# Two raw input tiles transposed by a DMA from DRAM instead of on TensorE, in a gated mixer and MLP block

## The chip, the cores and the metric

The kernel runs on one core of one Trainium2 chip. A core has five engines with instruction queues of their own: TensorE (PE: matrix products and transposes, results in PSUM), VectorE (DVE), ScalarE (ACT), GpSimd (POOL) and SyncE (SP, which here only issues DMAs); sixteen DMA engines carry out what SP and ACT issue. The metric is the device time of one execution in microseconds (us), lower is better. PEld is TensorE's weight load, which overlaps its products.

## The reference

The input x is 2048 by 512, in bf16. With LN a layer norm without gain or bias over the last axis, and gelu in its tanh form:

```python
h  = gelu(LN(x) @ w1)              # 2048x512 @ 512x512
# channel quarters of h: shifted along the sequence by +1, -1, +2, -2 rows, zeros moved in
hs = concatenate([g0, g1, g2, g3], axis=-1) @ w2
x1 = x + hs
y  = x1 + gelu(LN(x1) @ w3) @ w4   # w3 512x1792, w4 1792x512
```

## The kernel before, in words

The 2048 rows are 16 tiles of 128 (row p*16+t is partition p of tile t), so a shift along the sequence is a step from one tile to another. Each product needs its input with channels on partitions, so every tile has to be transposed once for w1 and once more, after the second layer norm, for w3.

Two sorts of tiles are treated differently in the first layer. Tiles 0 to 5 are "raw" (R = 6): x itself is transposed and multiplied by w1 (m1r), and the layer norm is put on afterwards, on the product, from the column sums of w1 (cs) and the statistics of the tile (zr, g1r); the result hraw is then transposed by a DMA (th_t, two tiles at a time, into hT). Tiles 6 to 15 are normed first (st: statistics, ag: their aggregation, rs: the root on POOL, nm: the norm on DVE), transposed and multiplied in pairs (m1p, then gelu g1p or g1s on ACT, straight into hT).

There are two ways of transposing. On TensorE, `tp` does four 128x128 transposes a tile against an identity (line 357) into PSUM, and `ev` copies the bank to xnT (line 366). By DMA, `tdma` (line 377; td0_t in the first layer, td1_t in the second) takes a pair of tiles from SBUF to SBUF, issued on SP. Before the change, raw tiles 0 to 5 and the pairs 8 and 10 went through TensorE, and pairs 6, 12 and 14 through the DMA.

Then m2 (lines 463 and 478, in parts) multiplies the shifted windows of hT by w2, DVE adds x (x1, line 488), and the second layer goes over the tiles in the order 8 to 15, 0 to 7 (ORDER), four at a time: m3h (first four, in halves, line 520) and m3 (line 496) with w3, gelu, m4 with w4 (line 539) and the last addition (fin). Tile t of m2 reads its neighbours: m2_14 and m2_15 read tiles 0 and 1 of hT too, which come out of th_0.

The order on each engine is written out by hand in `firsts`, one list of names per engine; `arrange` keeps each list, and `emit` puts waits only where a tile is read or overwritten. Every DMA has a semaphore of its own. What stands in a list is done in that order, so an operation that waits holds everything behind it on its engine. The lists that matter here:

- PE: the raw transposes and their m1r run interleaved from 4 us on; after m1r5 come tp8 m1p6 tp10 m1p8 m1p10, then parts of m2 for tiles 8 to 11, then m1p12, m1p14 and the rest of m2, and the first m3h.
- DVE: st0_10 and st0_11 stand ahead of nm0_8 and nm0_9, and st0_12 and st0_13 ahead of nm0_10 and nm0_11.
- SP: x and w1, w2 in the order of first use; td0_6 waits for nm0_7, td0_12 for nm0_13, td0_14 for nm0_15, th_0 for g1r1, td1_8 for nm1_9. The first halves of w3 (ldw3a0 to 3, 256 KB each) are loaded in pairs between these, the second halves (ldw3b, 192 KB each) after td1_8.

The kernel is straight-line code: nothing of it loops on the chip.

Of the kernel before, what the change touches and what calls it, by code (L numbers as in the profile page):

```python
# [26 lines left out]
class Program:  # L27
# [7 lines left out]
    def add(self, eng, name, fn, reads=(), writes=(), dma=False):  # L35
        self.ops.append(Op(name, eng, fn, reads, writes, dma))
# [135 lines left out]
def bass_standalone__mixer_s_mlp__prompt_kernel(nc: bass.Bass, x, w1, w2, w3, w4, out):  # L172
# [10 lines left out]
    xd = x[0].rearrange("(p t) d -> p t d", t=NT)  # L183
# [4 lines left out]
    with ExitStack() as es:  # L188
# [5 lines left out]
        xnT = sb("xnT", [P, NT, DC, P], BF16)  # L194
# [52 lines left out]
        add = pr.add  # L247
# [4 lines left out]
        def bres(b, n, tag):  # L252
            return [(("ps", b + i), tag) for i in range(n)]
# [19 lines left out]
        def load_x(t, n, eng="sp"):  # L273
            add(eng, f"ldx{t}", lambda e: e.dma_start(x_sb[:, t : t + n, :], xd[:, t : t + n, :]),
                writes=[(("x", i), 0) for i in range(t, t + n)], dma=True)
# [72 lines left out]
        def tp(t, n, b, raw):  # L348
            src = x_sb if raw else xn
            rd = [(("x", i), 0) if raw else (("xn", i), 0) for i in range(t, t + n)]  # L350

            def f(e):
                ins = None
                for i in range(n):
                    for c in range(DC):
                        o = 1024 * b + (i * DC + c) * P
                        ins = e.transpose(psb[:, o : o + P], src[:, t + i, P * c : P * (c + 1)], ident[:])  # L357
                return ins

            add("pe", f"tp{t}", f, reads=rd + [("ident", 1)], writes=bres(b, 1, f"tp{t}"))  # L360

        def ev(t, n, b, eng="act"):
            src = psb[:, 1024 * b : 1024 * b + n * D]
            dst = xnT[:, t : t + n, :, :].rearrange("p t c s -> p (t c s)")
            if eng == "act":
                f = lambda e: e.activation(dst, src, ACT_F.Copy)  # L366
            else:
                f = lambda e: e.tensor_copy(dst, src)
            add(eng, f"ev{t}", f, reads=bres(b, 1, f"tp{t}"), writes=[(("xT", i), 0) for i in range(t, t + n)])


        def tdma(layer, t, n):
# [6 lines left out]
                reads=[dst_of(layer, i)[2:] for i in range(t, t + n)],  # L379
                writes=[(("xT", i) if layer == 0 else ("x1T", i), 0) for i in range(t, t + n)], dma=True)  # L380

        def tdma_h(t, n):
            add("sp", f"th_{t}",
                lambda e: e.dma_start(hT[:, t : t + n, :, 0:P].rearrange("p t j w -> p (t j) w"),
                                      hraw[:, t : t + n, :].rearrange("p t d -> p (t d)"), transpose=True),
                reads=[(("hraw", i), 0) for i in range(t, t + n)],
                writes=[(("hT", i), 0) for i in range(t, t + n)], dma=True)
# [13 lines left out]
        def m1r(t, b, c0=0, c1=DC):  # L401
            def f(e):
                ins = None
                for c in range(c0, c1):
                    ins = e.matmul(bank(b), xnT[:, t, c, :], w1_sb[:, c, :], start=(c == 0), stop=(c == DC - 1))  # L405
                return ins

            rd = [(("xT", t), 0)] + W1[c0:c1]
            if c0:
                rd += bres(b, 1, f"m1r{t}{c0}")  # L410
            end = f"{c1}" if c1 < DC else ""
            add("pe", f"m1r{t}{end}", f, reads=rd, writes=bres(b, 1, f"m1r{t}{end}"))

        def rc(t, b):
            add("act", f"rc{t}", lambda e: e.activation(yraw[:, t, :], bank(b), ACT_F.Copy),
                reads=bres(b, 1, f"m1r{t}"), writes=[(("yraw", t), 0)])
# [169 lines left out]
        load_w1(2, "act")  # L586
        load_w1(3, "sp")
        load_x(1, 1, "act")
        for t, n in ((6, 1), (7, 1), (2, 1), (8, 1), (3, 1), (9, 1), (10, 1), (4, 1), (11, 1), (5, 1), (12, 2), (14, 1), (15, 1)):
            load_x(t, n)  # L590
        for c in range(DC):
            load_w2(c)
# [7 lines left out]
            colsum(4, c)  # L600
        colsum_out(4)
        for t in range(R):
            tp(t, 1, 6 + t % 2, True)
            ev(t, 1, 6 + t % 2, "act")
            cuts = [0, 1, 2, 3, 4] if t == 0 else [0, 2, 4] if t == 1 else [0, 4]
            for c0, c1 in zip(cuts, cuts[1:]):
                m1r(t, YB[t], c0, c1)
            rc(t, YB[t])
# [37 lines left out]
        for t in range(0, R, 2):  # L646
            roots(0, t, 2)
            for i in (t, t + 1):
                zr(i)
                g1r(i)  # L650
            tdma_h(t, 2)
        for t in (8, 10):
# [7 lines left out]
            tdma(1, t, 2)  # L660

        firsts = {}
        firsts["pe"] = """wu tp0 cs0 cs1 m1r01 m1r02 tp1 m1r03 m1r0 cs2 tp2 m1r12 m1r1 cs tp3 m1r2 tp4 m1r3 tp5 m1r4 m1r5 tp8 m1p6
            tp10 m1p8 m1p10 m2_8a m2_9a m2_8 m2_9b m2_9 m2_10a m2_11a m1p12 m1p14 m2_10 m2_11 m2_12a m2_13a m2_12 m2_13 m2_14 m2_15""".split()
        firsts["act"] = """ldw10 ldw12 ldx1 table ev0 ev1 ev2 rc0 ev3 rc1 ev4 rc2 ev5 rc3 rc4 rc5 ev8 cse g1p6 ev10 g1p8 g1s10 g1s11
            g1r0 g1r1 g1p12 g1p14 g2h_0_0_0 g2h_0_0_4 g1r2 g1r3 g2h_0_0_8 g2h_0_0_12 g1r4 g1r5""".split()
        firsts["dve"] = """pada padb padc padd pade padf st0_0 st0_6 st0_7 ag0_6 ag0_7
            st0_8 nm0_6 nm0_7 st0_9 ag0_8 ag0_9 st0_10 st0_11 nm0_8 nm0_9 ag0_10 ag0_11
            st0_12 st0_13 nm0_10 nm0_11 ag0_12 ag0_13 st0_14 nm0_12 nm0_13 st0_15 ag0_14 ag0_15 st0_1 ag0_0 ag0_1
            nm0_14 nm0_15 zr0 zr1 x1_8 x1_9 st1_8 st1_9 ag1_8 ag1_9 st0_2 nm1_8 nm1_9 st0_3 ag0_2 ag0_3 x1_10 x1_11 st1_10  # L670
            st1_11 ag1_10 ag1_11 x1_12 nm1_10 nm1_11 x1_13 x1_14 x1_15 zr2 zr3 st0_4 st0_5 ag0_4 ag0_5 zr4 zr5
            st1_12 st1_13 ag1_12 ag1_13""".split()
        firsts["pool"] = """ident0 ident1 neghalf stz ste rs0_6 rs0_8 rs0_10
            rs0_12 rs0_14 rs0_0 rs1_8 rs0_2 rs1_10""".split()
        firsts["sp"] = """ldx0 ldw11 ldw13 ldx6 ldx7 ldx2 ldx8 ldx3 ldx9 ldx10 ldx4 ldx11 ldx5 ldx12 td0_6 ldx14 ldx15 ldw20 ldw21 ldw22 ldw23 td0_12 ldw3a0 ldw3a1 td0_14
            ldw3a2 ldw3a3 th_0 td1_8 ldw3b0 ldw3b1 ldw3b2 ldw3b3 td1_10 th_2 th_4 td1_12 td1_14 ldw4""".split()

        slots = [4, 0, 2]
        ns = [0]
# [110 lines left out]
```

## Time and profile before

| | |
|---|---|
| median of three runs | 137.16 us (136.78 to 137.19) |
| the profiled execution | 136.84 us, its span 134.9 us |
| TensorE busy | 131.8 us, 98% of the span, clock granted in full |
| DVE, ACT, POOL busy | 57.9, 47.6, 12.4 us |
| moved by DMA | 12.70 MB, of it 6.82 read from HBM and 2.10 written to it |
| 128x128 transposes on TensorE (L357) | 40: 24 of raw tiles, 16 of normed ones |

How to read it. The span goes from the first to the last instruction of the profiled execution. A group's line names the line of the kernel, engine, operation, what is written and read, and shapes. A matmul's busy time is longer than the distance to the next one, since they are pipelined: 128x512 products start 0.216 us apart and are shown as 0.379 long. The chain is followed back from the last instruction, from each to what released it. The DMA view gives for each issue the time from the issue to the landing, the moment at which the semaphore has its full count. A DMA share over 1 means more than one open packet per DMA engine.

### The profile page before, as it was taken

Reading aid. Unit: us, or ns where it says so; the run is one execution under the profiler, and the core shown is the slowest. Engines: PE = TensorE matmul, PEld = TensorE weight load, DVE = VectorE, ACT = ScalarE, POOL = GpSimd, SP = SyncE. Lnnn points to the kernel's source line nnn. Section 1 sums busy time; section 2 is a strip of 40 time slices with the busy share of each in tenths; the row PEclk is TensorE's granted clock in tenths of the full one; section 3 lists DMA queues with packets and bytes.
Section 4 is the critical chain, followed back from the end, with each engine's and each line's share of the span. In section 5 each row is a group of like instructions: output and inputs, shape, how many; then the busy total and the mean of one; then the engine's idle time right before and its main releaser. Section 6 shows DMA issues by size and latency. Waiting matters only on the chain.

```text
span 134.9 us, 1823 instructions
## 1 busy us (share of the span) xinstructions
PE 131.8 (98%) x737; PEld 69.8 (52%) x737; DVE 57.9 (43%) x135; ACT 47.6 (35%) x58; POOL 12.4 (9%) x25
## 2 busy tenths in 40 slices
PE   7999999999999999999999999999999999999993
PEld 2356867568885444444444444444444444444452
DVE  0499979999866786772222000122200002322222
ACT  3489873407963025551000555200066630000000
POOL 2023422220420012220000000000000000000000
PEclk9999999999999999999999999999999999999999
DMA  3988589774466973444112000011110001111121
GB/s 104 332 264 189 151 228 251 132 222 83 77 119 119 290 256 66 92 78 78 39 48 70 3 0 0 0 39 39 39 39 5 0 0 39 39 39 39 41 78 41
DMA packets 23512, 12.70 MB, mean 94 GB/s; under 512 B 15696, under 2 KB 22864, under 8 KB 23504
## 3 DMA queue, kind: packets, MB, share of 16 engines
q1 hardware_dynamic: 22928, 12.16, 35.8%
q10 hardware_dynamic: 576, 0.43, 1.1%
q8 instruction: 6, 0.10, 0.3%
q14 instruction: 2, 0.02, 0.0%
HBM read 6.82 MB, written 2.10 MB: 66 GB/s over the span
## 4 chain that ended last, share of the span: by engine, by line
PE 98%; DVE 0%; issue 0%
PE ps L539 36%; PE ps L496 27%; PE ps L520 9%; PE ps L437 6%; PE ps L463 6%; PE ps L405 4%; PE ps L478 4%; PE ps L562 2%; PE ps L357 2%; PE ps L393 1%; DVE o_sb L551 0%
## 5 line engine op out<-in xcount | busy, mean ns | idle before, releaser
L539 PE MATMUL ps<-w_sb,h2T 128*128 128x512 bf16 (+2 forms) x238 | 48.9, 367 | 0.0
L507 ACT ACTIVATE h2T<-ps 128x1024 bf16<-128x1024 f32 x21 | 21.5, 1023 | 46.2 <-PE ps L496 46.2
L551 DVE TENSOR_TENSOR o_sb<-ps,x_sb 128x512 bf16<-128x512 f32 (+2 forms) x17 | 11.2, 660 | 61.2 <-PE ps L539 61.2
L496 PE MATMUL ps<-x1nT,w_sb 128*128 128x512 bf16 x168 | 36.8, 379 | 0.0
L539 PEld LDWEIGHTS ps<-w_sb,h2T 128*128 128x128 bf16 x238 | 22.7, 98 | 26.0
L496 PEld LDWEIGHTS ps<-x1nT,w_sb 128*128 128x128 bf16 x168 | 16.5, 98 | 19.8
L291 DVE BATCH_NORM_STATS2 st<-x_sb 128x6 f32<-128x512 bf16 x32 | 20.6, 676 | 4.1 <-DMA x_sb<-in_x_dram 4.1
L302 POOL TENSOR_TENSOR rstd<-mv,neghalf 128x2 f32<-128x2 f32 x16 | 11.5, 718 | 46.6 <-DVE mv L296 46.5
L520 PE MATMUL ps<-x1nT,w_sb 128*128 128x256 bf16 x112 | 12.4, 273 | 0.0
L488 DVE TENSOR_TENSOR x_sb<-ps,x_sb 128x512 bf16<-128x512 f32 x16 | 10.6, 685 | 3.1 <-PE ps L463 2.1
L520 PEld LDWEIGHTS ps<-x1nT,w_sb 128*128 128x128 bf16 x112 | 11.0, 98 | 1.5
L531 ACT ACTIVATE h2T<-ps 128x1024 bf16<-128x1024 f32 (+1 forms) x8 | 7.1, 913 | 6.6 <-PE ps L520 6.6
L437 PE MATMUL ps<-xnT,w_sb 128*128 128x256 bf16 x80 | 9.2, 273 | 0.0
L463 PE MATMUL ps<-w_sb,hTf 128*128 128x512 bf16 x40 | 9.0, 379 | 0.0
L437 PEld LDWEIGHTS ps<-xnT,w_sb 128*128 128x128 bf16 x80 | 7.7, 98 | 1.2
L311 DVE TENSOR_SCALAR x1n<-x_sb,mv,rstd 128x512 bf16<-128x512 bf16 x16 | 5.9, 410 | 5.3 <-POOL rstd L302 5.3
L366 ACT ACTIVATE xnT<-ps 128x512 bf16<-128x512 bf16 (+1 forms) x8 | 5.6, 702 | 2.5 <-PE ps L357 2.4
L463 PEld LDWEIGHTS ps<-w_sb,hTf 128*128 128x128 bf16 x40 | 3.9, 98 | 4.5
L405 PE MATMUL ps<-w_sb,xnT 128*128 128x512 bf16 x24 | 6.2, 381 | 0.0
L478 PE MATMUL ps<-w_sb,hTf 128*128 128x512 bf16 x24 | 5.5, 379 | 0.0
L447 ACT ACTIVATE hTf<-ps 128x1024 bf16<-128x1024 f32 x4 | 4.1, 1023 | 3.4 <-PE ps L437 3.4
L296 DVE BATCH_NORM_AGGREGATE mv<-st 128x2 f32<-128x9 f32 x32 | 4.9, 184 | 0.0
(28 smaller groups left out, 37.2 us busy)
## 6 DMA issues: line engine op xcount, KB each, us to landing
out_dram<-o_sb SPq DMA_DIRECT2D x15, 128.0 KB, 1.8
w_sb<-in_w_dram SPq DMA_DIRECT2D x1, 1792.0 KB, 8.1
x_sb<-in_x_dram SPq DMA_DIRECT2D x13, 128.0 KB, 3.5
w_sb<-in_w_dram SPq DMA_DIRECT2D x4, 256.0 KB, 3.8
w_sb<-in_w_dram SPq DMA_DIRECT2D x6, 128.0 KB, 3.3
w_sb<-in_w_dram SPq DMA_DIRECT2D x4, 192.0 KB, 3.0
w_sb<-in_w_dram ACTq DMA_DIRECT2D x2, 128.0 KB, 3.5
x_sb<-in_x_dram SPq DMA_DIRECT2D x1, 256.0 KB, 3.5
```

Source lines behind the costliest of these rows:

```text
L291: add("dve", f"st{layer}_{t}", lambda e: e.bn_stats(st9[:, i, 0:6], src[:, t, :]), reads=[(r, 0)], writes=[(("st6", i), 0)])
L302: lambda e: e.tensor_tensor(rstd[:, i : i + n], mv[:, i : i + n, 1], neghalf[:, 0:n], ALU.pow),
L405: ins = e.matmul(bank(b), xnT[:, t, c, :], w1_sb[:, c, :], start=(c == 0), stop=(c == DC - 1))
L437: ins = e.matmul(dst, w1_sb[:, c, P * fc : P * (fc + 1)], xnT[:, t : t + 2, c, :], start=(c == 0), stop=(c == DC - 1))
L463: ins = e.matmul(bank(b), hTf[:, c0 : c0 + P], w2_sb[:, j, :], start=(j == 0), stop=(j == DC - 1))
L478: ins = e.matmul(bank(b), hTf[:, w[0] : w[0] + P], w2_sb[:, j, :], start=first and n == 0, stop=last and n == len(js) - 1)
L488: lambda e: e.tensor_tensor(x1_sb[:, t, :], bank(b), x_sb[:, t, :], ALU.add),
L496: ins = e.matmul(bank(b), w3_sb[:, c, P * fc : P * (fc + 1)], x1nT[:, 4 * q : 4 * q + 4, c, :], start=(c == 0), stop=(c == DC - 1))
L507: lambda e: e.activation(h2T[:, fc : fc + 2, q % 2, :], src, ACT_F.Gelu_apprx_tanh),
L520: ins = e.matmul(dst, w3_sb[:, c, P * (fc + i) : P * (fc + i + 1)], x1nT[:, t : t + 2, c, :], start=(c == 0), stop=(c == DC - 1))
L539: ins = e.matmul(ps[:, 512 * b : 512 * b + c1 - c0], h2T[:, fc, q % 2, P * i : P * (i + 1)], w4_sb[:, fc, c0:c1], start=(fc == 0), stop=(f ...
L551: lambda e: e.tensor_tensor(o_sb[:, k % 4, c0:c1], ps[:, 512 * b : 512 * b + c1 - c0], x1_sb[:, t, c0:c1], ALU.add),
```

## The change

Tiles 4 and 5 are no longer transposed on TensorE. One DMA on SP, `tdx_4`, reads the pair straight from x in DRAM and writes it transposed into xnT; tp4, tp5 and the copies ev4 and ev5 are gone. The untransposed tiles 4 and 5 (for their statistics and the addition in x1) are now loaded by one DMA of 256 KB far behind, ahead of td1_10. The other moves, all in the written orders:

- SP: tdx_4 stands behind ldx9, then ldx10, ldx11, td0_6. Tiles 12 to 15 are loaded behind td0_6, one by one (12 and 13 were one DMA ahead of it). td0_14 stands directly behind td0_12, ahead of all four first halves of w3 (it stood between the second and the third).
- DVE: nm0_10 and nm0_11 stand ahead of st0_12 and st0_13.
- PE and ACT: only the four names that are gone.

```diff
+        def tdma_x(t):
+            add("sp", f"tdx_{t}",
+                lambda e: e.dma_start(xnT[:, t : t + 2, :, :].rearrange("p t c s -> p (t c) s"),
+                                      xd[:, t : t + 2, :].rearrange("p t d -> p (t d)"), transpose=True),
+                writes=[(("xT", i), 0) for i in (t, t + 1)], dma=True)
...
-        for t, n in ((6, 1), (7, 1), (2, 1), (8, 1), (3, 1), (9, 1), (10, 1), (4, 1), (11, 1), (5, 1), (12, 2), (14, 1), (15, 1)):
+        for t, n in ((6, 1), (7, 1), (2, 1), (8, 1), (3, 1), (9, 1), (10, 1), (11, 1), (12, 1), (13, 1), (14, 1), (15, 1), (4, 2)):
             load_x(t, n)
...
         for t in range(R):
-            tp(t, 1, 6 + t % 2, True)
-            ev(t, 1, 6 + t % 2, "act")
+            if t < 4:
+                tp(t, 1, 6 + t % 2, True)
+                ev(t, 1, 6 + t % 2, "act")
+            elif t == 4:
+                tdma_x(t)
...
-        firsts["pe"] = """wu tp0 cs0 cs1 m1r01 m1r02 tp1 m1r03 m1r0 cs2 tp2 m1r12 m1r1 cs tp3 m1r2 tp4 m1r3 tp5 m1r4 m1r5 tp8 m1p6
+        firsts["pe"] = """wu tp0 cs0 cs1 m1r01 m1r02 tp1 m1r03 m1r0 cs2 tp2 m1r12 m1r1 cs tp3 m1r2 m1r3 m1r4 m1r5 tp8 m1p6
...
-        firsts["act"] = """ldw10 ldw12 ldx1 table ev0 ev1 ev2 rc0 ev3 rc1 ev4 rc2 ev5 rc3 rc4 rc5 ev8 cse g1p6 ev10 g1p8 g1s10 g1s11
+        firsts["act"] = """ldw10 ldw12 ldx1 table ev0 ev1 ev2 rc0 ev3 rc1 rc2 rc3 rc4 rc5 ev8 cse g1p6 ev10 g1p8 g1s10 g1s11
...
-            st0_12 st0_13 nm0_10 nm0_11 ag0_12 ag0_13 st0_14 nm0_12 nm0_13 st0_15 ag0_14 ag0_15 st0_1 ag0_0 ag0_1
+            nm0_10 nm0_11 st0_12 st0_13 ag0_12 ag0_13 st0_14 nm0_12 nm0_13 st0_15 ag0_14 ag0_15 st0_1 ag0_0 ag0_1
...
-        firsts["sp"] = """ldx0 ldw11 ldw13 ldx6 ldx7 ldx2 ldx8 ldx3 ldx9 ldx10 ldx4 ldx11 ldx5 ldx12 td0_6 ldx14 ldx15 ldw20 ldw21 ldw22 ldw23 td0_12 ldw3a0 ldw3a1 td0_14
-            ldw3a2 ldw3a3 th_0 td1_8 ldw3b0 ldw3b1 ldw3b2 ldw3b3 td1_10 th_2 th_4 td1_12 td1_14 ldw4""".split()
+        firsts["sp"] = """ldx0 ldw11 ldw13 ldx6 ldx7 ldx2 ldx8 ldx3 ldx9 tdx_4 ldx10 ldx11 td0_6 ldx12 ldx13 ldx14 ldx15 ldw20 ldw21 ldw22 ldw23 td0_12 td0_14 ldw3a0 ldw3a1
+            ldw3a2 ldw3a3 th_0 td1_8 ldw3b0 ldw3b1 ldw3b2 ldw3b3 ldx4 td1_10 th_2 th_4 td1_12 td1_14 ldw4""".split()
```

## The prediction

> **What bounds the kernel now.** I read the page's busy times, then the chain that ended last in order of time, then each engine's timeline of the first 31 us, then the DMA issues with their landing times in narrow windows. The profiled execution took 136.84 us outside and 134.9 us inside its span, so 1.94 us lie around the span. It is 0.32 us under the median of the three runs (137.16).
>
> ```profile
> PE 131.8 (98%) x737; PEld 69.8 (52%) x737; DVE 57.9 (43%) x135; ACT 47.6 (35%) x58; POOL 12.4 (9%) x25
> ```
>
> TensorE is the whole chain (PE 98%): there is no idle microsecond to win, only work to take off PE, and any new wait of PE is paid in full. The stretch that the change touches, in the chain in order of time (start, length, what):
>
> ```profile
> 8.08 0.22 PE ps L357 x4
> 8.30 0.86 PE ps L405 x4
> 9.17 0.31 PE ps L357 x4
> 9.48 0.86 PE ps L405 x4
> 10.34 0.22 PE ps L357 x4
> 10.57 1.73 PE ps L405 x8
> 12.29 0.45 PE ps L357 x8
> ...
> 27.11 1.73 PE ps L463 x8
> 28.84 1.20 PE ps L520 x11
> ```
>
> L357 are the transposes: four for raw tile 3, four for tile 4 (with a pause of 0.09 before them), four for tile 5, eight for the normed pair 8/9. Chain times carry the end of an instruction; on the timeline the same pieces start 0.16 earlier (tp8 at 12.13, m2_14 at 26.95, the first m3h at 28.68). I use timeline starts from here.
>
> VectorE is the engine just off the chain:
>
> ```profile
> 9.66 1.24 DVE L291 BATCH_NORM_STATS2 st<-x_sb 128x6 f32<-128x512 bf16 x2
> 10.82 0.72 DVE L311 TENSOR_SCALAR xn<-x_sb,mv,rstd 128x512 bf16<-128x512 bf16 x2
> 11.46 0.26 DVE L296 BATCH_NORM_AGGREGATE mv<-st 128x2 f32<-128x9 f32 x2
> 11.63 1.24 DVE L291 BATCH_NORM_STATS2 st<-x_sb 128x6 f32<-128x512 bf16 x2
> 12.79 0.72 DVE L311 TENSOR_SCALAR xn<-x_sb,mv,rstd 128x512 bf16<-128x512 bf16 x2
> ```
>
> Stats of tiles 10 and 11 stand ahead of norms 8 and 9, which end at 11.54; PE asks for them at 12.13. So a late x10 delays tp8.
>
> The third thing to see is that the DMA engines are full until 15 us, and what a transpose costs them (columns: window, PE, PEld, DVE, ACT, POOL busy, PE clock, DMA share, GB/s):
>
> ```profile
> 2.50:6.50 4.00, 3.98 (x19) 1.43 (x17) 1.36 (x3) 2.10 (x4) 0.00 (x0) 1.00 0.99 326
> 10.20:11.60 1.40, 1.40 (x11) 0.71 (x10) 1.40 (x6) 1.40 (x4) 0.32 (x1) 1.00 1.00 191
> 23.00:24.00 1.00, 1.00 (x11) 0.90 (x10) 0.77 (x4) 0.97 (x1) 0.25 (x1) 1.00 2.27 104
> ```
>
> Loads run at 326 GB/s, the transpose td0_6 (256 KB at 10.2 to 11.6) at 191. In 23 to 24 us, where th_0 is queued behind the w3 loads, packets are open (share 2.27) and little moves. Landings, each from the DMA view of its own window: x9, issued at 4.50, lands after 3.9 (8.4); td0_6, 8.94, 3.2 (12.1); w3a1, 17.47, 3.3 (20.8); td0_14, 17.95, 4.1 (22.05); w3a2, 19.23, 4.3 (23.5); w3a3, 19.85, 5.0 (24.9); th_0, 20.80, 5.1 (25.9); td1_8, 24.05, 3.1 (27.1). One queue, in order: a transpose behind loads lands 1.0 to 1.25 after the load ahead of it.
>
> **The change part by part.**
>
> *Step 1, off PE.* Eight transposes of 0.055 (0.22 per four) = 0.44, and the 0.07 to 0.09 pause ahead of tile 4. Most that can be won: 0.51. Two copies on ACT go too (x2 of 0.60); ACT is off the chain there, so nothing.
>
> *Step 2, tdx_4 lands.* It takes ldx10's place in SP's queue, at 4.97, waits for nothing, and stands behind x9. Issuing costs SP 1.24 to 1.56 (the three xnT transposes), so x10 and x11 are issued by 7.5 and td0_6, which waits for nm0_7 (8.91), is not held. No row shows a transpose that reads DRAM. Nearest rows: behind w3a1, td0_14 landed 1.25 later; behind w3a3, th_0 1.0 later. I take 1.25 on x9's 8.4: 9.6. Low end: as quick as two loads, which land 0.35 apart here (x2, x8, x3 and x10, x4, x11 by their windows), 9.0. High end: twice the 1.4 us of td0_6's stretch, 11.0. PE, without tp4 and tp5, asks at 9.87 (m1r3 from 9.0, 0.86), so m1r4 does not wait at 9.6.
>
> [...]
>
> *Step 3, x10 and x11 behind it.* x10 lands 0.4 after tdx_4, 10.0; st0_10 starts at 10.05 instead of 9.66, and nm0_9 ends 1.88 later (11.54 less 9.66), at 11.93. tp8 starts at 11.98 instead of 12.13: 0.15 is left of 0.51, and each tenth that tdx_4 lands later costs a tenth. Low and high: tp8 at 11.62 (PE's own, -0.51) and at 13.35 (+1.2). td0_6 (12.1) is there before m1p6 asks (12.43).
>
> *Step 4, DVE's new order.* nm0_10/11 go ahead of st0_12/13, because x12 lands only about 13.2 now (x14, issued at this place, took 2.9 from 10.33). rs0_10 ends 0.95 after nm0_9 (12.49 less 11.54), at 12.88, and nm0_11 at 13.64; tp10 asks at about 14.2. The two stats then add 1.16 behind it: nm0_13 ends at 16.5 (was 15.22), nm0_15 at 18.9 (17.59), zr1 at 20.2 (18.92). x1_8 starts at 20.25 instead of 19.77, as it had 0.85 of idle time ahead of it, and all of DVE after it is 0.4 late. Its users have room: the PSUM banks of x1_8 and x1_9 are asked for after 25. POOL's roots follow DVE (POOL is idle 46.5 us waiting for mv, nothing). ACT's g1r0 and g1r1 wait for zr0 and zr1 and end near 21.6; behind them g1p12 starts at 23, so nothing. On SP, x12 to x15 are issued from 10.33 to 12.3 behind td0_6, and w2 0.9 later, landing by 16.9 (asked for at 18.1).
>
> *Step 5, td0_12 and td0_14.* td0_12 is issued at 16.55 (was 15.25) and lands by 19.7; m1p12 asks at 20.9. td0_14 has no w3 load in front now: issued at 18.93, landed 3.1 later, 22.0, as before; m1p14 asks at 22.7. Hidden both. If the cover went (1.2 and 0.7), the rest is a wait of PE.
>
> *Step 6, what is late next: th_0.* All four w3a loads (1 MB) now stand between td0_14 and th_0, where two stood. They are issued from 20.2 to 22.2 (1.05 a pair), th_0 at 22.25. After td0_14 (22.0) the first lands 1.45 later (23.5, as w3a2 did), the next ones 0.9 to 1.4 apart (w3a0 to w3a1, w3a2 to w3a3), th_0 1.0 after the last: 27.2 with 0.9, 28.7 with 1.4, and with the megabyte at the 361 GB/s that the window of 22 to 23 shows (2.9 after 22.0) 25.9. Who needs it is m2_14, which reads tile 0 of hT and stands ahead of all the w3 products in PE's list; PE asks at 26.8. I take 27.2, the spacing in a stretch without the dead microsecond: m2_14 starts 0.3 later than before. td1_8, behind th_0, lands 1.25 after it, 28.45; the first m3h asks at 29.0. Of the rest, w3b and the late load of tiles 4 and 5 (256 KB, 0.6 of SP, landing near 31; st0_4 reads at 35.0) stand ahead of td1_10, which lands near 33 and is asked for at 35.
>
> *Sum.* PE gains 0.15 by tp8 and loses 0.45 at m2_14: +0.3 on the profiled 136.84 is 137.1, on the median 137.46; rounded, 137.4. After m2_14 PE runs closed to the end, so what it has lost or won there stays.
>
> **Rivals.**
> - *A, all hidden (faster).* tdx_4 is no dearer than the two loads it replaces in the queue, and lands at 9.0; x10 lands by 9.4, and all of 0.51 is won, if th_0 lands by 26.4: 136.65 by the median. It turns at 9.75 for the landing and 26.9 for th_0. For it: x4, x5, x12 and x13, half a megabyte, leave the queue ahead of td0_6. Against: the 191 GB/s, and the 1 MB ahead of th_0. [...]
> - *B, the DRAM source is slow (slower).* tdx_4 needs up to 2.7 us or meets one of the pauses of the early loads (6.5 to 8.5 runs at 256 GB/s against 326), lands at 10.2 to 11.0, m1r4 waits, and tp8 is 0.4 to 1.2 late: 137.6 to 138.4. For it: a transpose spreads over all engines and th_0 stood still for a microsecond behind one late load. Against: PE asks late, 9.87. A th_0 at 28.7 would cost 1.8 by step 6 and give 139.0; that end has 0.04 of this chance and is left out of the range.
>
> **Numbers.** Forecast (steps 3 and 6 as summed, between -0.2 and +0.6) 0.50; A 0.24; B 0.26. A measurement of this kernel can tell about 0.3% (0.41 us) from no change. A lies past 0.41 but for 0.02; of the forecast's half three tenths lie above +0.41 (0.15), and all of B: faster 0.22, same 0.37, slower 0.41. Range: from A's 136.65 to B's 138.4; the likeliest case's own is 136.95 to 137.8.
>
> **What would show it.** Step 1: sixteen raw transposes of L357 instead of twenty-four, no pause ahead of m1r4. Steps 2 and 3: tdx_4's landing time, PE waiting ahead of L405 for a DMA, VectorE's L291 waiting for x_sb near 10, tp8 at 11.6 to 12.0. Step 4: DVE's L488 starting near 20.2. Step 6: PE waiting at L463 near 27 for a DMA into hTf, and that DMA's time to landing near 5. The prediction is wrong if th_0 lands before 26.4, or if tdx_4 takes over 6 us from its issue.

## The result, and the profile after

The changed kernel took 137.87 us (median of 13 runs, 137.26 to 139.37), the kernel before 137.01 beside it: a ratio of 1.0065, 95% interval 1.0049 to 1.0081. The change made the kernel 0.9 us slower. The profiled execution took 137.82 us, its span 135.7, 0.8 more than before. Ratios here and below leave out the executions that lie over 1.5% above the fastest of their kernel (one of these thirteen).

The changed kernel's code lies seven lines further down from line 382 on: m1r is L412 (was L405), m1p L444 (L437), the first parts of m2 L485 (L478), whole m2 groups such as m2_14 L470 (L463), the first m3h L527 (L520). From the page, busy times and the chain by engine:

```profile
PE 131.1 (97%) x719; PEld 69.3 (51%) x729; DVE 58.2 (43%) x135; ACT 46.9 (35%) x56; POOL 12.4 (9%) x25
...
PE 93%; DMA 4%; issue 0%; DVE 0%
```

PE has less work, as step 1 said, and the chain is no longer all PE: 4% of it is one DMA. The chain in order of time names it:

```profile
20.72 1.66 PE ps L444 x16
22.38 5.34 DMA hTf<-hraw
27.73 0.04 issue
27.77 1.90 PE ps L470 x8
29.67 12.23 PE ps L527 x112
```

This is th_0, issued at 22.38 and landed 5.34 later, and m2_14 starts 0.04 after it. PE's timeline (start, length, what; in brackets the idle time before it):

```profile
7.81 0.39 PE L357 MATMUL ps<-ident,x_sb 128*128 128x128 bf16 x4
8.04 3.62 PE L412 MATMUL ps<-w_sb,xnT 128*128 128x512 bf16 x15
11.60 0.62 PE L357 MATMUL ps<-ident,xn 128*128 128x128 bf16 x8
...
20.56 1.91 PE L444 MATMUL ps<-xnT,w_sb 128*128 128x256 bf16 x16
22.80 1.92 PE L444 MATMUL ps<-xnT,w_sb 128*128 128x256 bf16 x16 [0.34 <-DMA xnT<-xn]
24.56 2.54 PE L485 MATMUL ps<-w_sb,hTf 128*128 128x512 bf16 x10
27.77 1.90 PE L470 MATMUL ps<-w_sb,hTf 128*128 128x512 bf16 x8 [0.67 <-DMA hTf<-hraw]
```

The same stretch before, from m1p12 on:

```profile
21.08 3.66 PE L437 MATMUL ps<-xnT,w_sb 128*128 128x256 bf16 x32
24.57 2.54 PE L478 MATMUL ps<-w_sb,hTf 128*128 128x512 bf16 x11
26.95 1.89 PE L463 MATMUL ps<-w_sb,hTf 128*128 128x512 bf16 x8
```

Four m1r run closed from 8.04 on without a wait for tdx_4, and tp8 starts at 11.60 (12.13 before). Two waits follow: m1p14 should start 1.75 after m1p12, at 22.31, and starts at 22.80, waiting for td0_14; m2_14 starts at 27.77, 0.83 after the work ahead of it ends by the times of before (26.95 less 24.57 is 2.38; 24.56 and 2.38 is 26.94). The idle times in brackets are 0.16 smaller, because the display shows the last product 0.38 long where the next could start after 0.22 (0.27 and 0.11 for the products of 128x256); waits are given below by the starts.

VectorE in the same profile:

```profile
12.52 0.74 DVE L311 TENSOR_SCALAR xn<-x_sb,mv,rstd 128x512 bf16<-128x512 bf16 x2 [0.80 <-POOL rstd L302]
13.40 1.29 DVE L291 BATCH_NORM_STATS2 st<-x_sb 128x6 f32<-128x512 bf16 x2 [0.15 <-DMA x_sb<-in_x_dram]
...
18.10 0.74 DVE L311 TENSOR_SCALAR xn<-x_sb,mv,rstd 128x512 bf16<-128x512 bf16 x2
18.76 1.40 DVE L427 SCALAR_TENSOR_TENSOR zraw<-ncs,mv,yraw 128x512 f32<-128x512 f32 x2
20.08 1.28 DVE L495 TENSOR_TENSOR x_sb<-ps,x_sb 128x512 bf16<-128x512 f32 x2
```

It now waits 0.80 for a root, with nothing put into that gap, and then 0.15 for x12; norms 14 and 15 start at 18.10, 1.24 later than before:

```profile
16.86 0.73 DVE L311 TENSOR_SCALAR xn<-x_sb,mv,rstd 128x512 bf16<-128x512 bf16 x2
```

With them td0_14 is issued 0.9 later (18.86, 17.95 before), and the first w3 load behind it too (20.14, 19.23 before); between td0_14 and th_0 stand four loads instead of two.

A way to add this up, used for every run below: three stretches of each profile, from PE's timeline. The first ends where the transposes of tile 3 start (the loads and PE's own start set it; it varies by itself from 7.7 to 8.8). The second, from there to the start of m1p6, holds what the DRAM transpose takes off PE, and any wait for td0_6. The third, from m1p6 to m2_14, holds the waits. From m2_14 to the end of the span it is 107.9 to 108.0 us in every profile.

| kernel | tile 3 starts | to m1p6 | m1p6 to m2_14 |
|---|---|---|---|
| before | 7.92 | 4.66 | 14.37 |
| changed | 7.81 | 4.24 | 15.72 |
| th_0 ahead of w3a2 (e1) | 7.74 | 4.35 | 14.66 |
| w3 in pairs again (e2) | 8.76 | 4.22 | 15.62 |
| w3 first (e3) | 8.35 | 4.16 | 14.72 |
| without the DRAM transpose (e4) | 8.32 | 4.58 | 15.03 |
| DRAM transpose alone (e5) | 8.16 | 4.27 | 14.38 |
| the same again (e5 again) | 8.18 | 4.61 | 14.39 |
| the same again (e10) | 8.30 | 4.12 | 14.37 |
| DRAM transpose, w3 in the changed order (e7) | 8.06 | 4.48 | 14.39 |
| DVE repaired and th_0 ahead (e11) | 8.38 | 4.21 | 14.62 |
| DVE repaired alone (e12) | 8.24 | 4.24 | 14.72 |
| DRAM transpose, x6 and x7 early (e8) | 8.16 | 4.34 | 15.07 |
| before, x6 and x7 early (e9) | 8.44 | 4.57 | 14.37 |

Before to changed: -0.11, -0.42 and +1.35, the 0.8 of the spans. In this profile the change wins nearly all that it takes off PE, and loses three times as much 10 to 15 us later.

### The profile page after: what moved, and what is told of

Its sections match the earlier page's. It is cut to its first block, busy times and chain, and to the rows that moved or that the text cites. A ratio compares the mean times of both kernels' runs of the same rounds, so it can differ in the third digit from the quotient of the medians.

```text
span 135.7 us, 1796 instructions
## 1 busy us (share of the span) xinstructions
PE 131.1 (97%) x719; PEld 69.3 (51%) x729; DVE 58.2 (43%) x135; ACT 46.9 (35%) x56; POOL 12.4 (9%) x25
## 4 chain that ended last, share of the span: by engine, by line
PE 93%; DMA 4%; issue 0%; DVE 0%
PE ps L546 35%; PE ps L503 27%; PE ps L527 9%; PE ps L470 6%; PE ps L444 5%; DMA hTf<-hraw 4%; PE ps L412 4%; PE ps L569 2%; PE ps L485 2%; PE ps L357 2%; PE ps L400 1%; DVE o_sb L558 0%
## 5 line engine op out<-in xcount | busy, mean ns | idle before, releaser
L546 PE MATMUL ps<-w_sb,h2T 128*128 128x512 bf16 (+2 forms) x232 | 48.1, 366 | 0.3
L527 PE MATMUL ps<-x1nT,w_sb 128*128 128x256 bf16 x112 | 12.4, 273 | 0.0
L527 PEld LDWEIGHTS ps<-x1nT,w_sb 128*128 128x128 bf16 x112 | 11.0, 98 | 1.5
L444 PE MATMUL ps<-xnT,w_sb 128*128 128x256 bf16 x80 | 9.4, 273 | 0.3 <-DMA xnT<-xn 0.3
L470 PE MATMUL ps<-w_sb,hTf 128*128 128x512 bf16 x39 | 8.8, 379 | 0.7 <-DMA hTf<-hraw 0.7
L444 PEld LDWEIGHTS ps<-xnT,w_sb 128*128 128x128 bf16 x80 | 7.6, 98 | 1.8 <-DMA xnT<-xn 0.6
L470 PEld LDWEIGHTS ps<-w_sb,hTf 128*128 128x128 bf16 x40 | 3.8, 98 | 5.4 <-DMA hTf<-hraw 1.2
L412 PE MATMUL ps<-w_sb,xnT 128*128 128x512 bf16 x23 | 5.9, 384 | 0.1
L485 PE MATMUL ps<-w_sb,hTf 128*128 128x512 bf16 x22 | 5.2, 379 | 0.1
L366 ACT ACTIVATE xnT<-ps 128x512 bf16<-128x512 bf16 (+1 forms) x6 | 4.4, 738 | 2.3 <-PE ps L357 2.3
```

The lines of the kernel that those rows point to most:

```text
L444: ins = e.matmul(dst, w1_sb[:, c, P * fc : P * (fc + 1)], xnT[:, t : t + 2, c, :], start=(c == 0), stop=(c == DC - 1))
L470: ins = e.matmul(bank(b), hTf[:, c0 : c0 + P], w2_sb[:, j, :], start=(j == 0), stop=(j == DC - 1))
L485: ins = e.matmul(bank(b), hTf[:, w[0] : w[0] + P], w2_sb[:, j, :], start=first and n == 0, stop=last and n == len(js) - 1)
L527: ins = e.matmul(dst, w3_sb[:, c, P * (fc + i) : P * (fc + i + 1)], x1nT[:, t : t + 2, c, :], start=(c == 0), stop=(c == DC - 1))
L546: ins = e.matmul(ps[:, 512 * b : 512 * b + c1 - c0], h2T[:, fc, q % 2, P * i : P * (i + 1)], w4_sb[:, fc, c0:c1], start=(fc == 0), stop=(f ...
```

## The experiments

Theory: the loss is th_0, late behind a megabyte of w3 that stands behind the late td0_14. Rivals: the DRAM transpose itself; the later order of DVE whatever w3 does; the order of w3 whatever DVE does. Each ratio is to the runs of the kernel before on the same chip.

**e1: th_0 ahead of half of the megabyte.**

```diff
-            ldw3a2 ldw3a3 th_0 td1_8
+            th_0 ldw3a2 ldw3a3 td1_8
```

> The changed kernel with th_0 issued ahead of ldw3a2 and ldw3a3; nothing else differs. Theory (the loss is m2_14 waiting for th_0, which stands behind 1 MB of w3): th_0 is issued near 21.4 us and lands by 25.5 instead of 27.7, the wait of 0.8 us ahead of m2_14 goes, m1p14's wait of 0.5 for td0_14 stays, and td1_8 lands near 28.2, just before PE asks at 28.7: 0.8 us less than the changed kernel, 137.0 us or a ratio of 1.000 to before. Rival (the loss is made earlier, by the DRAM transpose and the moved x loads, and th_0 only shows it): PE then waits elsewhere, and the time stays above 137.5 us.

Measured: 137.04 us, ratio 1.0014 (0.9985 to 1.0043). PE's timeline:

```profile
20.60 3.95 PE L444 MATMUL ps<-xnT,w_sb 128*128 128x256 bf16 x32
24.38 2.54 PE L485 MATMUL ps<-w_sb,hTf 128*128 128x512 bf16 x10
26.75 1.89 PE L470 MATMUL ps<-w_sb,hTf 128*128 128x512 bf16 x8
```

No wait stands ahead of L470: th_0 was issued at 21.04 and landed 4.3 later. m1p14's wait is in the 3.95 (3.66 before). Moving one name in one list gives back about 0.7 us by the ratios. The interval is wide, but its upper end, 1.0043, lies below the lower one of the changed kernel, 1.0049. m1p14 still waits 0.3.

**e2: two w3 loads back between td0_12 and td0_14.**

```diff
-td0_12 td0_14 ldw3a0 ldw3a1
+td0_12 ldw3a0 ldw3a1 td0_14
```

> The changed kernel with ldw3a0 and ldw3a1 put back between td0_12 and td0_14, as before the change. Theory: half a megabyte of w3 is moved at 18 to 20.5 us, where the DMA engines stand idle in the changed kernel; th_0 lands near 26 and m2_14 does not wait; td0_14, issued at 18.9 behind the two loads, lands at 22.3 to 22.9, so m1p14 waits up to 0.6. Together 136.7 to 137.1 us, ratio 0.998 to 1.001. Rival (DVE's later order is what costs, through td0_14's issue at 18.9): at least 137.4 us.

Measured: 137.96 us, ratio 1.0069 (1.0043 to 1.0095). The expectation failed: m2_14 no longer waits, but m1p14 does, for 1.2 us by the starts. (The profiled execution took 138.64 us, 0.7 over the median.)

```profile
21.49 1.91 PE L444 MATMUL ps<-xnT,w_sb 128*128 128x256 bf16 x16
24.47 1.92 PE L444 MATMUL ps<-xnT,w_sb 128*128 128x256 bf16 x16 [1.07 <-DMA xnT<-xn]
26.23 2.54 PE L485 MATMUL ps<-w_sb,hTf 128*128 128x512 bf16 x10
28.60 1.89 PE L470 MATMUL ps<-w_sb,hTf 128*128 128x512 bf16 x8
```

td0_14 landed 4.6 after its issue, where I had said 3.4 to 4.0, and was issued a microsecond later than I had reckoned in this execution, with all early loads late (tile 3 at 8.76). This kernel has w3 in the order of before and loses as much as the changed one. So the changed order of td0_14 and w3 is not what costs: with norms 14 and 15 late, td0_14 pays in the one order and th_0 in the other.

**e4: the changed orders without the DRAM transpose.** The DMA of tiles 4 and 5 loads them untransposed in tdx_4's place, and tp4, tp5, ev4 and ev5 are back.

```diff
-ldx9 tdx_4 ldx10
+ldx9 ldx4 ldx10
...
-cs tp3 m1r2 m1r3 m1r4 m1r5
+cs tp3 m1r2 tp4 m1r3 tp5 m1r4 m1r5
```

> The changed kernel without its DRAM transpose: tiles 4 and 5 are loaded (256 KB) in the place of tdx_4 and transposed on TensorE as before the change; the order of x12 to x15, of DVE and of w3 stays the changed one. Theory: tp8 starts at 12.1 again, m1p14 no longer waits, but th_0 lands near 27.5 all the same, because DVE's norms of 14 and 15 and the w3 loads set it; m2_14 starts at 27.5 to 27.8 and the time stays within 0.3 us of the changed kernel, 137.6 to 137.9 us, ratio 1.004 to 1.007. Rival (the DRAM transpose costs): it falls to 137.0 us.

Measured: 137.61 us, ratio 1.0028 (1.0012 to 1.0045), below the 1.004 that I had as the low end.

```profile
24.89 2.54 PE L485 MATMUL ps<-w_sb,hTf 128*128 128x512 bf16 x10
27.93 1.90 PE L470 MATMUL ps<-w_sb,hTf 128*128 128x512 bf16 x8 [0.51 <-DMA hTf<-hraw]
```

th_0 landed 5.5 after its issue at 22.42 and m2_14 started at 27.93, whatever PE had won or not won before. Without the DRAM transpose the kernel is still slower than before. That the DRAM transpose is the whole loss is refuted. It is not shown to be free inside the changed order: the two intervals (1.0012 to 1.0045 and 1.0049 to 1.0081) do not overlap, though they come from two sets of runs. In the profiles m1p14 does not wait in e4, where PE arrives later, and m2_14 waits 0.66 instead of 0.83; what brought the ratio below the 1.004 was not isolated.

**e5, e5 again, e10: the DRAM transpose alone.** The kernel before, with tdx_4 in the place of ldx10; x12 and x13, DVE and w3 as before.

```diff
-ldx9 ldx10 ldx4 ldx11 ldx5 ldx12 td0_6
+ldx9 tdx_4 ldx10 ldx11 ldx12 td0_6
...
-ldw3b3 td1_10
+ldw3b3 ldx4 td1_10
```

> The kernel before with the DRAM transpose alone: tiles 4 and 5 transposed by tdx_4 behind ldx9, their plain load ahead of td1_10; x12 and x13 stay ahead of td0_6, DVE's order and w3's order stay those of before. Theory: tp8 starts at 11.6; td0_6 stands behind 0.3 us more of traffic and lands near 12.3, so m1p6 starts at 12.1 to 12.35; nothing later waits, as th_0 lands near 25.9: 0.2 to 0.5 us faster than before, ratio 0.9965 to 0.9985. Rival (the DRAM transpose delays x10 to x13 and the rest of DVE): 137.0 us or more.

> The kernel with the DRAM transpose alone a second time, for a profile, since 4 of its 12 times lay 1.5 to 2.5 us above the others and none of 35 times of the kernel before did. Theory (one late DMA ring among the early loads holds the whole transpose and everything queued behind it): in a long execution x9 lands near 9 us instead of 8.1, tdx_4, x10 and x11 follow a microsecond late, and tp8 waits on DVE. Rival (something late in the kernel): the first 13 us look alike. In a short one, 136.5 to 136.9 us, neither is told apart.

> The kernel with the DRAM transpose alone once more, timed, as the yardstick of the two runs beside it. Theory: m1p6 waits for td0_6 at 12.4 to 12.8, so the 0.5 us taken off PE are worth 0.0 to 0.2: 136.8 to 137.0 us, ratio 0.998 to 1.000. Rival (0.5 us are won in the usual execution and long executions hide it): 136.5 us in most of the times.

Measured: 136.90 us, ratio 0.9999 (0.9965 to 1.0033), then a single 137.08, then 136.87, ratio 0.9995 (0.9982 to 1.0007). Four of the first twelve times lay at 138.3 to 139.1, which widens that interval; none of the second twelve did, and the single profile fell among the usual ones, so what makes a long execution was not seen. In the profile of e10:

```profile
11.98 0.61 PE L357 MATMUL ps<-ident,xn 128*128 128x128 bf16 x8
12.42 1.91 PE L443 MATMUL ps<-xnT,w_sb 128*128 128x256 bf16 x16
...
26.79 1.89 PE L469 MATMUL ps<-w_sb,hTf 128*128 128x512 bf16 x8
```

Here all 0.54 us are won (4.12 against 4.66) and nothing waits later. Yet the medians move by 0.1 to 0.2 only, and the ratios by less. In three others of these profiles PE does wait, for td0_6: it landed at 12.39 in e5, at 12.75 in e5 again and at 12.50 in e7, and m1p6 started 0.04 to 0.05 after. With 0.5 us less work PE arrives at 12.3 to 12.4, just as td0_6 does. td0_6 was issued at 9.06 to 9.25 in these four and landed 3.2 to 3.5 later, and that decides what is left: e5 and e5 again differ by 0.03 in the issue and by 0.36 in the landing. The expectation of e10 (0.0 to 0.2) held, that of e5 (0.2 to 0.5) did not by its ratio.

**e7: the same, with w3 in the changed order.**

```diff
-td0_12 ldw3a0 ldw3a1 td0_14
+td0_12 td0_14 ldw3a0 ldw3a1
```

> The kernel before with the DRAM transpose and with w3 in the changed order (td0_14 directly behind td0_12, the megabyte ahead of th_0), but x12 and x13 loaded ahead of td0_6 and DVE's order as before. Theory (the loss needs both: norms 14 and 15 that are 1.2 us late, and the w3 loads behind td0_14): nm0_15 ends near 17.7, td0_14 is issued at 17.9 and lands near 21, the w3 loads follow at 19.2, th_0 lands at 25.6 to 26.3, asked for at 26.5: 136.7 to 137.0 us, as with the DRAM transpose alone. Rival (the order of w3 alone makes th_0 late): 137.5 us or more, with a wait ahead of m2_14.

Measured: 136.88 us, ratio 0.9993 (0.9983 to 1.0003).

```profile
24.55 2.54 PE L484 MATMUL ps<-w_sb,hTf 128*128 128x512 bf16 x11
26.93 1.89 PE L469 MATMUL ps<-w_sb,hTf 128*128 128x512 bf16 x8
```

With the norms at their old times the megabyte ahead of th_0 costs nothing: th_0, issued at 21.18, landed 5.6 later, at 26.83, just ahead of m2_14's 26.93. That is a tenth of a microsecond of room, in a profile in which PE had waited 0.3 for td0_6. Four of the kernels with the DRAM transpose now make a table:

| ratio to before | w3 as before | w3 in the changed order |
|---|---|---|
| x12 to x15 and DVE as before | 0.9995 (e10) | 0.9993 (e7) |
| x12 to x15 and DVE as changed | 1.0069 (e2) | 1.0065 (changed) |

The expectation's "the loss needs both" is therefore wrong, though its number held. The later x12 to x15 with DVE's new order, which make norms 14 and 15 late, cost about 0.9 us in either of these two orders of w3. The changed order of w3 has th_0 land about 1.0 later (25.86 before), which the room hid; it only moves the wait of the late norms from m1p14 to m2_14. The later x12 to x15 and DVE's new order were not run apart from each other; e12 below shows what DVE's order alone can give back.

**e3: two w3 loads into the idle time ahead of td0_12.**

```diff
-td0_12 td0_14 ldw3a0 ldw3a1
+ldw3a0 ldw3a1 td0_12 td0_14
```

> The changed kernel with ldw3a0 and ldw3a1 issued ahead of td0_12, directly behind the loads of w2, where SP and the DMA engines idle from 16.5 to 17.6 us; td0_14 follows td0_12, then ldw3a2, ldw3a3 and th_0 as in the changed kernel. Theory (th_0 is late for the megabyte between td0_14 and it): td0_12 lands at 19.8 to 20.2, asked for at 20.6; td0_14 lands as in the changed kernel, 22.0 to 22.8, and m1p14 waits up to 0.5; th_0 lands by 26.0 and m2_14 does not wait: 136.6 to 137.1 us, ratio 0.997 to 1.001. Rival (DVE's later order costs whatever the loads do): 137.5 us or more.

Measured: 137.07 us, ratio 1.0012 (0.9999 to 1.0025). m2_14 does not wait; m1p12 starts on time, 0.2 after td0_12 lands, and m1p14 waits 0.3 for td0_14. Moving the same half megabyte early instead of behind th_0 does the same good, so it is the queue ahead of th_0 and no other property of e1.

**e11 and e12: DVE's order repaired.** st0_1 goes into the gap of 0.80, st0_15 and the aggregations of 14 and 15 go ahead of norms 12 and 13; e11 has th_0 early too.

```diff
-            nm0_10 nm0_11 st0_12 st0_13 ag0_12 ag0_13 st0_14 nm0_12 nm0_13 st0_15 ag0_14 ag0_15 st0_1 ag0_0 ag0_1
-            nm0_14 nm0_15 zr0 zr1
+            st0_1 nm0_10 nm0_11 st0_12 st0_13 ag0_12 ag0_13 st0_14 st0_15 ag0_14 ag0_15 nm0_12 nm0_13
+            nm0_14 nm0_15 ag0_0 ag0_1 zr0 zr1
```

> The changed kernel with th_0 ahead of ldw3a2 and ldw3a3, and with DVE's order repaired: st0_1 goes into the 0.8 us in which DVE waits for the root of 10 and 11, st0_15 and the aggregations of 14 and 15 go ahead of norms 12 and 13, so that nm0_15 ends near 17.9 instead of 18.8. Theory: td0_14 is issued near 18.3, behind td0_12, and lands near 21.4, so m1p14 (asking at 22.3) no longer waits; th_0 lands by 25.5; from m1p6 to the end of the span 122.3 us, as in the kernel before, and from the transposes of tile 3 to m1p6 4.2 to 4.4 instead of 4.66: 136.6 to 136.8 us, ratio 0.997 to 0.9985. Rival (the DRAM transpose itself brings waits that no order repairs): 137.0 us or more.

> The changed kernel with DVE's repaired order alone, th_0 still behind the megabyte of w3. Theory: td0_14 0.6 earlier, the w3 loads from 19.5, th_0 lands near 27.0, so m2_14 still waits, 0.2 to 0.5 us; m1p14 does not: 136.9 to 137.3 us, ratio 0.999 to 1.002, between the changed kernel and the one with th_0 early. Rival (late norms are the whole loss): 136.6 us, as with th_0 early. Rival (the order of the w3 loads is the whole loss): 137.6 us or more.

Measured: e11 136.89 us, ratio 0.9985 (0.9967 to 1.0004); e12 137.28 us, ratio 1.0009 (0.9987 to 1.0030). In e12 td0_14 landed 3.5 after its issue, m1p14 did not wait, and m2_14 waited 0.3 for th_0, which landed 5.3 after its issue: earlier norms take away m1p14's wait and part of the other. x12 to x15 and w3 stand there as in the changed kernel, and most of the loss is gone (1.0009 against 1.0065), so DVE's order is where most of it can be had back. In e11 neither waits; its m1p6 to m2_14 is still 0.25 over 14.37. That lies between m1p10 and the first m2, where PE's weight loads pause for 0.34 us and the profile names nothing that they wait for. Of the versions with the changed order of x12 to x15 e11 is the best, but its interval takes in 1.

**e8 and e9: x6 and x7 ahead of ldw13**, with the DRAM transpose alone (e8) and in the kernel before (e9), to bring td0_6 forward.

```diff
-ldx0 ldw11 ldw13 ldx6 ldx7 ldx2
+ldx0 ldw11 ldx6 ldx7 ldw13 ldx2
```

> The kernel with the DRAM transpose alone, and x6 and x7 loaded ahead of ldw13 instead of behind it. Theory (with tp4 and tp5 gone, m1p6 waits for td0_6, whose start is the load of x6 and x7 and 5.7 us of DVE, POOL and DMA behind it: m1p6 started 0.04 to 0.07 after td0_6's landing in four profiles): x7 lands near 6.1, td0_6 near 12.1 instead of 12.4 to 12.75, m1p6 starts at 12.1 to 12.2; w13 lands near 6.4 and holds m1r0 by up to 0.25. Together 0.2 to 0.4 less than with the DRAM transpose alone: 136.5 to 136.7 us, ratio 0.996 to 0.998. Rival (m1p6 is held by something else): no change against the DRAM transpose alone, ratio 0.999 to 1.001.

> The kernel before with x6 and x7 loaded ahead of ldw13, and no DRAM transpose: the control. Theory: PE is the chain, so earlier norms win nothing, and a wait for w13 at m1r0 costs 0 to 0.2: 136.9 to 137.2 us, ratio 1.000 to 1.0015. Rival (the earlier loads win by themselves): under 136.7 us.

Measured: e8 137.14 us, ratio 1.0014 (0.9995 to 1.0032), a miss; e9 137.07 us, ratio 1.0008 (0.9995 to 1.0020), as expected. In e8 td0_6 was issued at 8.80 but landed 3.7 later, at 12.45, behind x12 and x13, which had landed at 11.25 only; m1p6 started at 12.50. td0_6's landing held m1p6 as the theory has it, but the queue ahead of td0_6 set that, not x6 and x7. m1p14 then waited 0.7 for a td0_14 that landed 5.1 after its issue. No version that ran is faster than the kernel before by more than its interval.

## Why the prediction was right, and where its steps were wrong

The forecast was 137.4 us, 0.25 to 0.3 slower than before, with 136.65 to 138.4 as the range; measured were 0.9 more than before. The sign holds, and so does the wait that step 6 named: m2_14 waits for th_0 behind a megabyte of w3. But the size was three times the forecast, outside the likeliest case's own range (136.95 to 137.8). 137.87 lies in the range as a whole only because that reached up to rival B's 138.4, and nothing of rival B happened: that the range held it was luck. Step 6 put the wait down to the w3 order, with td0_14 landing as before. That order costs nothing by itself (e7) and saves nothing when it is put back (e2), though others do (e1, e3): what the kernel loses by is the late norms.

- *Step 1* (0.51 off PE): right. Tile 3 to m1p6 fell from 4.66 to 4.24, in e10 to 4.12.
- *Step 2* (tdx_4 at 9.6): it landed at 9.1. The distance behind x9 was 1.1, within the 1.0 to 1.25 of the rows; x9 itself was earlier, 8.0 instead of 8.4. In the eleven profiles with tdx_4 the distance was 1.03 to 1.11, between the two SBUF rows (0.98 and 1.26), and the slow source of rival B did not appear. If the distance is all its own time, 256 KB (262,144 bytes) went at an estimated 236 to 254 GB/s, above the 191 of the stretch with td0_6 in the kernel before. No run transposes the same tiles from both sources.
- *Step 3* (tp8 at 11.98, 0.15 won): wrong in size. x10 landed at 9.6 and x11 at 9.9, st0_10 and st0_11 started when DVE was free, as before, and tp8 started at 11.60: 0.53 won. The step took the late end of tdx_4 and passed it on in full. Its second half, td0_6 there "before m1p6 asks", held by 0.14 (11.91 and 12.05), because x12 and x13 had been moved behind td0_6; with them ahead of it, td0_6 is the next bound, at 12.4 to 12.75 in four profiles (e5, e5 again, e7, e8).
- *Step 4*: right to a tenth. nm0_13 ended at 16.46 (16.5), nm0_15 at 18.84 (18.9), zr1 at 20.16 (20.2), x1_8 started at 20.08 (20.25).
- *Step 5* (td0_14 lands at 22.0, hidden): the issue was right, 18.86, the landing 3.9 later instead of 3.1, at 22.76. Its cover of 0.7 went to nothing, since PE had also come 0.38 earlier than step 3 said; m1p14 waited 0.49. I had taken 3.1 from transposes with nothing ahead of them, and the one with loads ahead of it (4.1) as their fault. Over all fourteen profiles td0_14 took 3.1 to 5.1, and in two of them only less than 3.4.
- *Step 6* (th_0 at 27.2): it landed at 27.73. The four loads landed at 23.45, 24.1, 26.1 and 26.7: the first 0.7 behind td0_14 instead of 1.45, two spacings of 0.65 to 0.7, one of 1.95, and th_0 1.0 behind the last. Together that is 4.97 behind td0_14, less than the 5.2 of the forecast, so here the whole lateness of th_0 is td0_14's 0.76. How the extra time falls differs: in e7 td0_14 landed after 3.1, and th_0 5.9 behind it. From td0_14's issue to th_0's landing it was 8.7 to 9.0 in all four profiles with this order (changed, e4, e7, e12), against 8.3 in the forecast. So 0.4 to 0.7 of the dead microsecond that I had left out came in each, in one place or another. m2_14 waited 0.83 instead of 0.45.
- *Sum*: -0.15 + 0.45 was forecast; the profile has -0.53 (of it 0.11 from the start, which varies by itself) + 0.49 + 0.83. Only one of these numbers decides, since m2_14 starts when th_0 is there, whatever PE has won or lost ahead of it: 27.77 instead of 27.25 is the whole error of the sum in this profile, and what PE won came back as waiting. e1 shows m2_14's part, e2 and e7 that the late norms make the loss in either order of w3, e4 that a part of it is there without the DRAM transpose.
- *Rival A* (all hidden) failed on th_0, as its own condition, landing by 26.4, had it. Its other half, tdx_4 no obstacle to x10, came true (x10 landed at 9.6, and tp8 started at 11.60).

What stays open: the long executions of e5; what the later x12 to x15 cost apart from DVE's order; how much the DRAM transpose costs inside the changed order (e4); why td0_14, with no load ahead of it, landed 3.89 after its issue in the changed kernel and 3.92 in e1 (the last section has what the profiles show); and 0.25 us in e11.

## What to carry to other kernels

When PE is the whole chain, taking half a microsecond off it is worth only what the next arrivals allow (from tile 3 to m1p6 e10 won 0.54 us, e5 again, where td0_6 landed at 12.75, 0.05): list, for each later product, when its input lands and how long before it is asked for, and treat a tenth of a microsecond of room, which is what th_0 had in e7, as none. When one engine's results come later, every transfer that waits for them moves along (here norms 14 and 15 came 1.24 later, and td0_14 was issued 0.9 later), and an order of loads around them that was harmless stops being so (e2), while another can take most of the loss away (e1, e3); look for the transfer at the end of the queue and ask which product reads it first. And size queued transfers by the rows with pauses in them, not by the best ones.

## What the runs showed of the hardware

A transpose that reads DRAM in 256 KB landed 1.03 to 1.11 us after the load ahead of it, in eleven profiles; transposes from SBUF behind a load landed 0.98 and 1.26 after it in the kernel before. I had given a slow DRAM source a quarter of the chance.

While td0_14 and th_0 are in the queue of the changed kernel, there are stretches in which packets are open (shares of 1.29 and 0.72) and little moves, 64 and 49 GB/s (columns: window, PE, PEld, DVE, ACT, POOL busy, PE clock, DMA share, GB/s):

```profile
20.10:21.10 1.00, 1.00 (x8) 0.68 (x7) 1.00 (x3) 0.82 (x2) 0.00 (x0) 1.00 1.21 215
21.10:22.00 0.90, 0.90 (x11) 0.80 (x9) 0.90 (x3) 0.00 (x0) 0.00 (x0) 1.00 1.29 64
22.00:23.50 1.50, 1.16 (x12) 0.81 (x10) 1.35 (x4) 1.00 (x1) 0.64 (x1) 1.00 1.08 356
...
25.50:26.50 1.00, 0.95 (x5) 0.41 (x5) 1.00 (x3) 0.28 (x1) 0.43 (x1) 1.00 0.72 49
```

The first slow stretch, 64 GB/s at a share of 1.29, falls into td0_14, and the DMA view of 20.5 to 22.5 has one transfer of another queue in it:

```profile
q14 instruction: 1, 0.01, 1.0%
```

The second, 49 GB/s, falls where the third w3 load is still landing and th_0 is behind it.

A DMA's semaphore gets sixteen counts in the traces, and their times tell more. Fifteen counts of that third load came from 24.61 to 25.28 and the last at 26.07. In e1, e3 and e8 fifteen counts of td0_14 came within 0.2 us and the last 0.83 to 0.88 later; in e1 the fifteenth was there 3.1 after the issue, the last 3.9. An 8 KB transfer of the instruction queue started while td0_14 was on its way in each of these three (21.2, 21.7 and 21.3) and in the changed kernel (20.8). In e7, where it started at 21.49, after td0_14 had landed, td0_14 took 3.1; but in e11 it started at 21.18, with td0_14 on its way, and td0_14 took 3.2. In the changed kernel itself all sixteen counts of td0_14 came late together (22.58 to 22.76). So in e1, e3 and e8 the last 0.83 to 0.88 us before td0_14's landing, and in the changed kernel the last 0.79 before that of the third w3 load, are one late count of sixteen. That the 8 KB transfer makes it late, and in the changed kernel held td0_14 as a whole, is my guess: it fits most of these profiles, not all, and no run here moved that transfer on purpose.
